# Hashed attention and a gated MLP on one core: feature rows moved to 51 to 76, the broadcast of the inverted sums in two transfers, and a new order

## The chip, the cores and the metric

The kernel runs on one core of a Trainium2 chip. The metric is the device time of one execution in microseconds (us). TensorE is PE in the profile, VectorE is DVE, ScalarE is ACT, GpSimd is POOL, and SyncE (SP) here does nothing but issue DMAs.

## The reference, cut to what matters

Each of 4 x 8 heads has 768 positions with 64 features. A position attends only to those whose six sign bits of a projection agree with its own. The result, with the heads side by side, goes through a gated MLP.

```python
q_bits = (np.einsum('bhsd,dk->bhsk', q, proj) > 0)      # and k_bits; 6 bits each
mask = q_bucket[:, :, :, None] == k_bucket[:, :, None, :]
scores = np.where(mask, scale * np.matmul(q, k.transpose(0, 1, 3, 2)), -1e9)
attn = np.exp(scores - np.max(scores, axis=-1, keepdims=True))
attn = attn / (np.sum(attn, axis=-1, keepdims=True) + 1e-09)
x = np.matmul(attn, v)                                  # to [b, 768, 512]
h = gelu(x @ w_in); u, v = h[..., :512], h[..., 512:]
out = x + (u * (w_sg @ layernorm(v, g_ln) + b_sg)) @ w_out
```

## The kernel before

**Attention.** The 32 heads are worked on as 16 pairs. The two heads of a pair lie on partitions 0 to 63 and 64 to 127, so that two matmuls over 64 rows run beside each other. For each pair:

- `load` brings q and k from HBM (L493). `parts` transposes them on PE (L529); ACT writes the high part `h` (L533) and a whole copy `x` (L542), DVE the low part `l` (L536).
- `bits` multiplies `x` by a projection `pn` on PE (L570), DVE turns the signs into features `fb` (L573), and DMAs on SP's queue carry them into the feature tile `f` (L580): eight transfers of 13 rows each, one for each of q and k, half of the positions, and head.
- `largest` makes scores with features on PE (L599) and takes row maxima on DVE (L607, L609); `shift` reduces them (`m`, L617), and small DMAs put them into one row of `f` for each head (L627).
- `weigh` makes the scores again, in nine units (L652); ACT takes the exponential into `p` (L657); PE multiplies by v (L675, L678); POOL adds the `p` up into `sum` (L687).
- `finish` comes twice for a pair, for 256 and for 512 positions: PE totals the sums (L708), ACT writes `sm` (L711), a DMA stores it to DRAM (`s`, L717), a second spreads it over partitions (`sq`, L718), DVE inverts it (L719), a third stores that (`r`, L721), and a fourth broadcasts it to `rs` (L722). Each of these waits for the one before. Then ACT (L728) and POOL (L729) read `rs`, DVE makes `xt` (L730), and a DMA stores it to `xs` in DRAM.

**MLP.** Products for the hidden layer (L901), for the gate (L1170) and for the output (L1216), from and to DRAM copies of the intermediate results.

**Order.** Each engine runs its instructions in the order in which the program gives them, and waits on semaphores. That order is made when the program is built: `Plan.order` takes every group of instructions with a priority, an assumed duration and, for DMAs, an assumed latency (`lat`), and places the group that it believes ready first. The many constants at the top are priorities and assumptions of that kind. An ACT or POOL instruction that waits for `rs` therefore holds up everything behind it on its engine.

The broadcast before is one DMA with two heads, 64 partitions each and n positions:

```python
dma(prio, 0.6, lambda eng: eng.dma_start(rs()[:, :n], rd.unsqueeze(1).broadcast_to([2, D, n])), [rb], [rs], lat=4.6 + trip)
```

At the start, `pr` (the projection) is loaded on POOL's queue (L313); ACT scales it into `pw` (L424), and `pwh`, `pwl` and `pn` follow. The six columns `fcol` come out of small matmuls (L415) and a copy on DVE (L416). Matmuls of the identity (L740) fill PE while it would stand still at the start.

Of the kernel before, what the change touches and what calls it, by code (L numbers as in the profile page):

```python
# [9 lines left out]
F32 = mybir.dt.float32  # L10
# [8 lines left out]
DRAM = bass.MemoryType.DRAM  # L19


MX = {'r0n': 3, 'zn': 3.6, 'base': 340.0, 'gs': False, 'norm': 'DVE', 'mul': ('DVE', 'DVE', 'POOL', 'POOL', 'DVE', 'POOL', 'POOL', 'POOL'), 'wg': -6.28, 'z0': -5.58, 'ox': -66.68, 'oz': -10.14, 'sp': -10.68, 'ro': -8.45, 'gr': -5.61, 'lx': 4.73, 'lz': -3.11, 'gap': 12.5, 'wo': -28.82, 'ws': 15.65, 'ul': 20.36, 'wi': -132.86, 'x0': -110.0, 'lox': ('POOL', 'DVE', 'DVE', 'DVE', 'DVE', 'POOL', 'POOL'), 'loz': ('DVE', 'POOL', 'DVE', 'POOL', 'POOL', 'POOL', 'POOL'), 'log': ('DVE', 'POOL', 'DVE', 'POOL'), 'low': ('POOL', 'DVE', 'POOL', 'DVE', 'DVE', 'DVE', 'DVE'), 'grb': 1, 'wob': 1, 'wj': -40.0}

AVP = 9.57
TRIP = 1.5
RAWS, LATEQ, PRQ = 2, 4.39, True
GY, GX, NPT = (3,), (3, 3), 14
NAV = 1
S0P = 0.76
AHEAD = 8  # L30
PREP, SHIFTP, FINP, WSTEP, WP = 0.43, -0.57, 2.66, 14.6, 17.17
LOADS = "SP"
ADDS = (["POOL", "POOL"], ["POOL", "POOL", "POOL", "POOL", "POOL"])
TAILP = -1.15
FIRSTP, FIRSTS, FIRSTQ, LATE = -3.35, 3.11, -7.41, 9.44
LOAD0 = 1.35
PARTP = 0.39
OPS = 3
VP, MARK, WARMUP = -20.0, 2, 30
X0P = 321.77  # L40
LASTADDS = ['DVE', 'POOL', 'DVE', 'DVE', 'DVE']
AHEAD1 = 3.03
BITP, BITL, FZP, XB = -16.85, 4.0, 1.42, 1
JOB0, JOBS, JOBL = 1, 108, 6.0
LOADW = 7.8
SHIFTL = 3.2
# [2 lines left out]
class Plan:  # L49
# [10 lines left out]
    TURN = 4.7  # L60
    STAY = 1.09
    BACK = 6.5
    SIDE = 1.99
    LAND = 0.62
    TAIL = {"DVE": 0.075, "ACT": 0.1, "POOL": 0.06}

# [23 lines left out]
        b.slots = slots  # L90
        return b

    def add(self, engine, cost, prio, fn, r=(), w=(), dma=0, port=None, form=None, lat=0.0):

        port = engine == "POOL" if port is None else port
        g = {"e": engine, "c": cost, "p": prio, "fn": fn, "dma": dma, "n": len(self.groups), "slots": [], "port": port, "form": form, "lat": lat}
# [24 lines left out]
        self.groups.append(g)  # L121

    def order(self):
        G = self.groups
# [31 lines left out]
        while len(out) < len(G):  # L156
# [72 lines left out]
            for m in users[n]:  # L229
                need[m] -= 1  # L230
                if n in G[m]["deps"]:
                    at[m] = max(at[m], (end if g["dma"] else free[e]) if G[m]["e"] == e and not g["dma"] else end + self.WAIT)
# [16 lines left out]
def kernel(  # L249
# [57 lines left out]

    BL, MROW = 64, 0  # L310
# [6 lines left out]

    frow = setup.tile([1, 6, P], F32, name="frow")
    nc.vector.memset(frow, 0.0)
    fv = frow[:, 0:4].rearrange("a f (b c) -> a f b c", c=BL)  # L320
    FR = 1 + NFE
    for s in range(2):
        for r in range(2):
            c0 = 1 + NB * r
            nc.vector.memset(fv[:, 2 * s, :, c0:c0 + NB], TINY if r == s else -TINY * (1.0 + 2.0 ** -23))
            nc.vector.memset(fv[:, 2 * s + 1, :, c0:c0 + NB],
                             (1.0, MISS)[s] * (1.0 if r == 0 else -1.0) * (1.0, -1.0)[s])
    nc.vector.memset(fv[:, 2, :, MROW:MROW + 1], -1.0)
    nc.vector.memset(fv[:, 3, :, MROW:MROW + 1], 1.0)
    for s in range(2):  # L330
        for f in range(2):
            for h in range(2):
                nc.gpsimd.tensor_copy(frow[:, 4 + f, 64 * s + 32 * h:64 * s + 32 * h + 2 * FR].rearrange("a (j r) -> a j r", j=2),
                                      fv[:, 2 * s + f, :, 0:FR])


    fcol = const.tile([P, 6], F32, name="fcol")

# [78 lines left out]
    pw = setup.tile([P, 2, P], F32, name="pw")  # L417
    nc.vector.memset(pw, 0.0)
    for s in range(2):
        pv = pw[:, s, :].rearrange("p (b c) -> p b c", c=BL)  # L420
        for j in range(2):
            for r in range(2):
                c0 = 1 + NB * r
                nc.scalar.mul(pv[j * D:(j + 1) * D, j, c0:c0 + NB], pr[j * D:(j + 1) * D], 1.0 if r == s else -1.0)  # L424
    pwh = const.tile([P, 2, P], F32R, name="pwh")
    pwl = const.tile([P, 2, P], F32R, name="pwl")
    nc.scalar.copy(pwh, pw)
    nc.gpsimd.tensor_sub(pwl, pw, pwh.bitcast(F32))
    pn = const.tile([P, 2, 32], F32, name="pn")
    nc.gpsimd.memset(pn, 0.0)  # L430
    for j in range(2):
        nc.gpsimd.tensor_copy(pn[j * D:(j + 1) * D, :, FR * j:FR * j + FR], pw[j * D:(j + 1) * D, :, BL * j:BL * j + FR])
# [10 lines left out]
    if True:  # L443
# [33 lines left out]
        def row(j):  # L477
            return slice(j * D, (j + 1) * D)
# [4 lines left out]
        def load(n, prio):  # L483
# [34 lines left out]
        def parts(st, i, prio):  # L518
# [3 lines left out]
            def at(t):  # L522
                return two(t()) if i == 0 else t()[:, :WIDE]
# [38 lines left out]
        def bits(st, prio):  # L562
# [50 lines left out]
        def shift(st, ph, prio):  # L613
# [78 lines left out]
        def finish(st, ph, prio):  # L692
# [599 lines left out]
```

## Time and profile before

| | |
|---|---|
| median of 3 runs | 728.65 us (725.12 to 729.06) |
| the profiled execution | 727.2 us, of which its span is 725.4 us |
| busy PE | 697.7 us, 96% of the span |
| busy DVE, POOL, ACT | 492.5, 410.4 and 384.4 us (68%, 57%, 53%) |
| DMA | 88.44 MB, mean 122 GB/s |
| longest parts of the chain that ended last | PE 65%, DMA 11% (`rs<-r` 6%), DVE 7% |

The span is from the first to the last instruction of the profiled execution; the device time around it is 1.8 us longer. Busy time of an engine counts each stretch in which at least one of its instructions runs. "Idle before" is what an engine waited before an instruction, with the instruction or DMA that ended the wait behind an arrow.

### The profile page before, as it was taken

To read this page: it belongs to the slowest core of one execution; us is meant where nothing else is said; L and a number is where in the kernel's file an instruction comes from. 1 tells how busy PE (TensorE), PEld (TensorE's weight loads), DVE (VectorE), ACT (ScalarE), POOL (GpSimd) and SP (SyncE) were. 2 spreads that over 40 slices of the span, in tenths; PEclk is the share of its full clock that TensorE was granted. 3 is DMA by queue.
4 is the path that set the end of the run, shared out by engine and by line. 5 is a ranking of instruction groups with operands and counts; after the bars stand their busy time and mean duration, and the time that the engine had idled before them with its cause. 6 is when DMAs were issued, how large, how long until landed. Compare 5 with 4: busy or idle time off the path is not lost.

```text
span 725.4 us, 16743 instructions
## 1 busy us (share of the span) xinstructions
PE 697.7 (96%) x6318; PEld 552.9 (76%) x6318; DVE 492.5 (68%) x920; ACT 384.4 (53%) x742; POOL 410.4 (57%) x371
## 2 busy tenths in 40 slices
PE   8999899899999998998998998999999999999997
PEld 7767566666665855765665658999999989899996
DVE  4987667677697676967755767748777966464343
ACT  3466456566575656665755656757668413232010
POOL 3377569668688867776966862222236553426040
PEclk9999999999999999999999999999999999999999
DMA  7523434334343344342125112799783776565433
GB/s 172 104 48 95 100 83 111 83 95 115 93 109 87 101 108 101 86 108 63 50 62 143 29 46 66 209 286 252 214 292 116 185 191 144 127 190 103 137 72 102
DMA packets 182848, 88.44 MB, mean 122 GB/s; under 512 B 148184, under 2 KB 162160, under 8 KB 182768
## 3 DMA queue, kind: packets, MB, share of 16 engines
q1 hardware_dynamic: 179600, 86.58, 45.5%
q10 hardware_dynamic: 3104, 0.80, 0.6%
q8 instruction: 50, 0.82, 0.5%
q14 instruction: 30, 0.25, 0.1%
q0 software_dynamic: 64, 0.00, 0.0%
HBM read 59.48 MB, written 25.36 MB: 117 GB/s over the span
## 4 chain that ended last, share of the span: by engine, by line
PE 65%; DMA 11%; DVE 7%; issue 6%; ACT 5%; POOL 3%; SPq 1%; ACTq 0%; POOLq 0%; DVEq 0%
PE g L1170 14%; PE g L652 13%; PE g L901 10%; PE g L1216 9%; PE g L599 6%; DMA rs<-r 6%; PE av L678 4%; PE av L675 4%; DMA sq<-s 2%; POOL sum L687 2%; ACT p L657 2%; PE g L529 2%; PE ftp L740 1%; PE g L708 1%; PE g L570 1%
## 5 line engine op out<-in xcount | busy, mean ns | idle before, releaser
L657 ACT ACTIVATE p<-g 128x512 f32<-128x512 f32 x288 | 157.0, 600 | 63.1 <-PE g L652 61.1
L687 POOL TENSOR_TENSOR sum<-sum,p 128x512 f32<-128x512 f32 x154 | 179.7, 1201 | 7.7 <-ACT p L657 7.6
L607 DVE TENSOR_REDUCE mx<-g 128x1 f32<-128x512 f32 x192 | 123.0, 684 | 22.1 <-PE g L599 18.1
L687 POOL TENSOR_TENSOR sum<-p,p 128x512 f32<-128x512 f32 x62 | 79.5, 1301 | 52.0 <-ACT p L657 52.0
L1170 PE MATMUL g<-w,op 128*128 128x384 f32 x576 | 100.6, 334 | 0.0
L1170 PEld LDWEIGHTS g<-w,op 128*128 128x128 f32 x576 | 100.0, 188 | 0.2
L675 PE MATMUL av<-p,v 128*32 128x512 f32 x768 | 88.0, 594 | 0.0
L652 PE MATMUL g<-h 64*128 64x256 f32 (+1 forms) x384 | 78.1, 358 | 6.5 <-ACT p L657 2.3
L599 PE MATMUL g<-f 64*128 64x512 f32 (+1 forms) x384 | 72.6, 348 | 1.6 <-DVE wflat L371 0.9
L652 PE MATMUL g<-f 64*128 64x256 f32 (+1 forms) x384 | 71.9, 336 | 1.9 <-DMA f<-m 1.9
L652 PE MATMUL g<-h,l 64*128 64x256 f32 (+1 forms) x384 | 73.2, 340 | 0.0
L609 DVE TENSOR_REDUCE mx<-g 128x2 f32<-128x512 f32 x96 | 61.8, 683 | 15.2 <-PE g L599 12.6
L652 PE MATMUL g<-l,h 64*128 64x256 f32 (+1 forms) x384 | 71.9, 336 | 0.0
L599 PE MATMUL g<-h 64*128 64x512 f32 (+1 forms) x384 | 70.1, 339 | 0.0
L729 POOL TENSOR_TENSOR xt<-un,rs 128x256 f32<-128x256 f32 (+1 forms) x32 | 32.5, 1016 | 59.5 <-DMA rs<-r 36.1
L901 PEld LDWEIGHTS g<-w,op 128*128 128x128 f32 x504 | 61.6, 191 | 4.3 <-issue 1.3
L901 PE MATMUL g<-w,op 128*128 128x256 f32 x504 | 63.1, 284 | 1.5 <-DVE xt L730 0.8
L652 PEld LDWEIGHTS g<-h 64*128 64x128 f32 x384 | 43.4, 187 | 27.4 <-issue 4.9
L901 PE MATMUL g<-op,w 128*128 128x384 f32 x336 | 60.3, 335 | 1.1 <-ACT out L1051 0.6
L1216 PE MATMUL g<-woh,op 128*128 128x512 f32 x192 | 60.0, 390 | 0.0
L901 PEld LDWEIGHTS g<-op,w 128*128 128x128 f32 x336 | 57.9, 188 | 1.8 <-ACT out L1051 0.9
L675 PEld LDWEIGHTS av<-p,v 128*32 128x32 f32 x768 | 23.6, 110 | 46.5 <-issue 44.4
(138 smaller groups left out, 1208.8 us busy)
## 6 DMA issues: line engine op xcount, KB each, us to landing
v<-in_v_dram SPq DMA_DIRECT2D x16, 384.0 KB
raw<-xs SPq DMA_DIRECT2D x16, 384.0 KB
vn<-out SPq DMA_DIRECT2D x24, 256.0 KB
ud<-out SPq DMA_DIRECT2D x16, 384.0 KB
ul<-ud SPq DMA_DIRECT2D x32, 192.0 KB
stg<-xs SPq DMA_DIRECT2D x96, 64.0 KB
raw<-vn SPq DMA_DIRECT2D x8, 768.0 KB
out_dram<-out SPq DMA_DIRECT2D x24, 256.0 KB
```

What stands on the lines that cost most here:

```text
L599: nc.tensor.matmul(sc[j]()[:, c * NY:c * NY + b - a], x()[row(j), 0, qs], x()[row(j), 1, a:b], start=(n == 0), stop=(n == 1))
L607: nc.vector.tensor_reduce(mx()[:, 0, i0 + w, j:j + 1], sc[j]()[:, :WIDE], axis=AX.X, op=ALU.max, negate=True)
L609: nc.vector.tensor_reduce(mx()[:, 1, i0:i0 + 2, j], two(sc[j]()), axis=AX.X, op=ALU.max, negate=True)
L652: nc.tensor.matmul(sc[j]()[:, i * w:(i + 1) * w], x()[row(j), 1, ks], y()[row(j), 0, cs], start=(m == 0), stop=(m == 3))
L657: plan.add(ACT, 0.6, prio, lambda j=j: nc.scalar.activation(p[j]()[:, :, :NY], two(sc[j]()), AF.Exp, scale=SCALE), [sc[j]], [p[j]])
L675: nc.tensor.matmul(two(av())[rows(j, a)], st.v()[:, j, x, cols(a)], ps[x][j]()[:, :, :NY], start=(x == 0), stop=(x == 5))
L678: nc.tensor.matmul(av()[rows(j, a), :NY + 1], st.v()[:, j, 2 * x + i, cols(a)], ps[x][j]()[:, i, :], start=(x == 0 and i == 0), stop=(x == ...
L687: (nc.gpsimd if e == POOL else nc.vector).tensor_add(two(sums[j]()), a, p[j]()[:, :, :NY])
L729: plan.add(POOL, 0.13 + n / 420.0, prio + TAILP, lambda: nc.gpsimd.tensor_mul(xt()[:, :n], un()[:, :n], rs()[:, :n]), [un, rs], [xt])
L901: nc.tensor.matmul(ps()[:, :n], lhs(s, i, ci, x, y), rhs(s, i, ci, x, y), start=(first and ci == 0 and x + y == 0), stop=(ci == nc_ - 1 an ...
L1170: nc.tensor.matmul(ps()[:, :HN], a()[:, x, c0:c0 + P], c()[:, 3 * HN * y + ci * HN:3 * HN * y + (ci + 1) * HN], start=(j == 0 and ci == 0 ...
L1216: nc.tensor.matmul(ps(), a()[:, x, c0:c0 + P], w()[:, 2 * j + ci, :], start=(j == 1 and ci == 0 and x == 0 and w is th), stop=(j == 0 and ...
```

## The change

- **Feature rows.** The features of the two heads lie in rows 51 to 63 and 64 to 76 of `f`, with the row of the maxima in 63 and 64, and no longer at 0 and at 64. A transfer of `bits` then takes both heads' 26 rows, so a pair needs four transfers of 26 rows and no longer eight of 13.
- **Broadcast.** `rs` is filled by two DMAs, one for each head, each from one row of `r` to 64 partitions. The second row of `f` and all sums are as before.
- **Setup.** `pw` and `pwh` are made on DVE and no longer on ACT. A small ACT instruction (`warm`) stands ahead of ACT's other work, and with it the load of the activation table.
- **Low part of pair 1** is subtracted on POOL (from `x`) and no longer on DVE.
- **Order.** The assumed latencies of the four DMAs of `finish` go from 3.6, 4.0, 4.0, 4.6 to 1.4, 2.6, 1.8, 3.2 us, consumers of `x` are assumed to wait 0.8 us longer, and some twenty priorities and engine choices have other values.

```diff
-MX = {'r0n': 3, 'zn': 3.6, 'base': 340.0, ...
+MX = {'r0n': 3, 'zn': 2.99, 'base': 340.0, ...
...
+LATS, XS = (1.4, 2.6, 1.8, 3.2), 0.8
...
+    FO, FR = D - 1 - NFE, 2 + 2 * NFE
...
-                nc.scalar.mul(pv[j * D:(j + 1) * D, j, c0:c0 + NB], pr[j * D:(j + 1) * D], 1.0 if r == s else -1.0)
+                c0 = (FO + NB - NB * r, D + 1 + NB * r)[j]
+                nc.vector.tensor_scalar_mul(pw[j * D:(j + 1) * D, s, c0:c0 + NB], pr[j * D:(j + 1) * D], 1.0 if r == s else -1.0)
...
-    nc.scalar.copy(pwh, pw)
+    nc.vector.tensor_copy(pwh, pw)
...
+                warm = late.ring([P, 1], F32, "warm")
+                plan.add(ACT, 1.4, prio + 0.5, lambda: nc.scalar.mul(warm(), small, 1.0), [], [warm])
...
+            if st.n in LOP:
+                plan.add(POOL, 1.28, prio + 0.2, low_s, [(t, x) for t in (st.x, hh) for x in keys], [(lo, x) for x in keys])
...
                     for h in range(2):
-                        for j in range(2):
-                            r = 64 * s + 32 * h + FR * j
-                            nc.sync.dma_start(ft()[j * D:j * D + FR, s, SH * h:SH * h + SH].bitcast(F32), fb()[r:r + FR, :].bitcast(F32))
-
-                plan.add(SP, 2.28, prio, spread, [fb], [(ft, (s, 0)), (ft, (s, 1))], dma=0.1, lat=BITL)
+                        r = 64 * s + 32 * h
+                        nc.sync.dma_start(ft()[FO:FO + FR, s, SH * h:SH * h + SH].bitcast(F32), fb()[r:r + FR, :].bitcast(F32))
+
+                plan.add(SP, 1.2, prio, spread, [fb], [(ft, (s, 0)), (ft, (s, 1))], dma=0.1, lat=BITL)
...
-            dma(prio, 0.6, lambda eng: eng.dma_start(rs()[:, :n], rd.unsqueeze(1).broadcast_to([2, D, n])), [rb], [rs], lat=4.6 + trip)
+            for j in range(2):
+                dma(prio, 0.6, lambda eng, j=j: eng.dma_start(rs()[row(j), :n], rd[j:j + 1].broadcast_to([D, n])), [rb], [(rs, j)], lat=LATS[3] + trip)
```

**What moves.** On SP's queue, where the broadcasts of pair 1's second half and of pair 2's first half are issued (a tile's number differs from build to build; `rs` of 512 is the second half), the order before is:

```order
L721 DMA r_1_204<-sq_1114 128x8
L718 DMA sq_1225<-s_0_205 128x4
L493 DMA k_1282<-in_k_dram 128x6x64
L722 DMA rs_1304<-r_1_204 128x1x512
L627 DMA f_199<-m_1285 1x128x2 x4
L721 DMA r_0_206<-sq_1225 128x4
L493 DMA q_1342<-in_q_dram 128x6x64 x2
L580 DMA f_200<-fb_1340 13x384 x4
L722 DMA rs_1395<-r_0_206 128x1x256
```

and of the change:

```order
L727 DMA r_1_201<-sq_1038 128x8
L361 DMA w_2_1124<-in_moe_w_in_dram 128x512
L723 DMA s_0_202<-sm_1155 4x128
L729 DMA rs_1159<-r_1_201 64x512 x2
L724 DMA sq_1187<-s_0_202 128x4
L727 DMA r_0_203<-sq_1187 128x4
L492 DMA k_1280<-in_k_dram 128x6x64
L492 DMA q_1299<-in_q_dram 128x6x64
L739 DMA xs_99<-xt_1255 128x512
L729 DMA rs_1310<-r_0_203 64x256 x2
```

Both broadcasts stand as two DMAs of 64 partitions; the first of them is now issued before the spread `sq` of the next half and before the loads of k and q, and the feature transfers have gone from between the two.

On PE, at the end of pair 2's second half (`av` is the product with v, `x` the copy that `bits` reads), the order before is:

```order
L675 MATMUL av_1287<-p_182,v_322 32x512 x2
L675 MATMUL av_1287<-p_183,v_322 32x512 x2
L570 MATMUL g_844_1320<-x_1302,pn 32x384 x4
L675 MATMUL av_1287<-p_170,v_322 32x512 x2
L675 MATMUL av_1287<-p_171,v_322 32x512 x2
```

and of the change:

```order
L681 MATMUL av_1284<-p_173,v_321 32x512 x2
L681 MATMUL av_1284<-p_174,v_321 32x512 x2
L714 MATMUL g_844_1343<-sum_1098,ones 32x256 x2
L714 MATMUL g_844_1343<-sum_1127,ones 32x256 x2
L578 MATMUL g_844_1351<-x_1297,pn 32x384 x4
```

The product for the bits has moved from the middle of the twelve `av` groups to behind all of them and behind the totals.

On DVE, at the start of the program (`p` and `mx` are tiles that are set to a constant), the order before is:

```order
L464 MEMSET mx_166 128x24
L468 MEMSET p_171 128x2
...
L468 MEMSET p_183 128x2
L416 COPY fcol<-ftp 128x6
L536 TENSOR_TENSOR l_0_306<-g_844_288,h_0_298 128x2x256
```

and of the change:

```order
L463 MEMSET mx_162 128x24
L424 TENSOR_SCALAR pw<-pr 64x6 x4
L463 MEMSET mx_163 128x24
...
L417 COPY fcol<-ftp 128x6
L424 TENSOR_SCALAR pw<-pr 64x6 x4
L427 CAST pwh<-pw 128x256
L538 TENSOR_TENSOR l_0_305<-g_844_287,h_0_297 128x2x256
```

The copy of `fcol` now stands behind the first four instructions that read `pr`.

## Rows read from the trace of the kernel before

**Rows 1.** Busy time by stage: us, each engine (instructions), PEclk, DMA share, GB/s.

```profile
25.00:425.00 400.00, 383.17 (x4381) 259.03 (x4381) 287.06 (x534) 244.86 (x485) 298.39 (x263) 0.99 0.35 88
425.00:450.00 25.00, 23.17 (x180) 16.98 (x176) 19.59 (x30) 15.97 (x31) 9.72 (x7) 1.00 0.11 33
450.00:725.00 275.00, 270.68 (x1598) 258.23 (x1597) 170.99 (x310) 115.03 (x208) 95.09 (x73) 1.00 0.64 176
```

**Rows 2.** Waits of PE from 25 to 425 us: total us, times, longest.

```profile
PE g L570 <- ACT x L542: 6.5, 9, 1.6
PE g L652 <- ACT p L657: 2.3, 2, 1.5
PE g L652 <- DMA f<-m: 1.9, 1, 1.9
PE g L652 <- DVE fb L573: 1.8, 2, 1.2
PE g L652 <- ACT sm L711: 1.6, 1, 1.6
```

**Rows 3.** Waits of the other engines from 25 to 425 us.

```profile
ACT g L728 <- DMA rs<-r: 49.0, 22, 5.6
...
DVE sq L719 <- DMA sq<-s: 23.3, 9, 4.0
```

**Rows 4.** Timeline, two broadcasts: start, duration in us, engine, line [idle before].

```profile
54.05 0.61 SPq L722 DMA_DIRECT2D rs<-r  x1
59.54 0.48 ACT L728 ACTIVATE g<-rs,less 128x256 f32<-128x256 f32 x1 [0.72 <-DMA rs<-r]
71.70 0.58 SPq L722 DMA_DIRECT2D rs<-r  x1
80.14 0.69 ACT L728 ACTIVATE g<-rs,less 128x512 f32<-128x512 f32 x1 [5.61 <-DMA rs<-r]
81.77 0.39 PE L652 MATMUL g<-h 64*128 64x256 f32 x1 [1.60 <-ACT sm L711]
```

**Rows 5.** Timeline, a small transfer issued behind a broadcast.

```profile
123.18 0.61 SPq L722 DMA_DIRECT2D rs<-r  x1
123.88 0.42 SPq L718 DMA_DIRECT2D sq<-s  x1
131.21 0.18 DVE L719 RECIPROCAL sq<-sq 128x4 f32<-128x4 f32 x1 [2.91 <-DMA sq<-s]
```

**Rows 6.** Busy time by stretch while that broadcast is under way.

```profile
127.00:128.00 1.00, 1.00 (x16) 0.27 (x10) 0.46 (x2) 1.00 (x3) 1.00 (x2) 1.00 0.84 178
128.00:130.50 2.50, 2.50 (x32) 0.91 (x28) 0.30 (x1) 0.65 (x2) 0.82 (x2) 1.00 0.19 44
```

**Rows 7.** Busy time in two stretches of lower granted clock, and before the second.

```profile
135.00:139.00 4.00, 3.25 (x23) 3.25 (x25) 3.48 (x8) 1.09 (x2) 1.20 (x2) 0.57 0.57 171
392.00:395.00 3.00, 1.06 (x6) 0.50 (x3) 0.03 (x1) 1.40 (x3) 1.33 (x2) 0.97 0.31 99
395.00:398.00 3.00, 3.00 (x17) 2.80 (x19) 2.77 (x5) 1.27 (x3) 2.28 (x2) 0.50 0.26 95
```

**Rows 8.** Timeline of PE, matmuls that wait for nothing.

```profile
78.71 0.29 PE L652 MATMUL g<-l,h 64*128 64x256 f32 x2
78.83 0.28 PE L652 MATMUL g<-f 64*128 64x256 f32 x2
```

**Rows 9.** Timeline of the start.

```profile
4.71 2.50 PE L740 MATMUL ftp<-ident 128*128 128x128 f32 x10 [0.26 <-DVE fcol L416]
5.04 1.28 ACT L424 ACT_TABLE_LOAD   x1 [5.04 <-DMA pr<-in_proj_dram]
...
19.69 0.80 DVE L557 TENSOR_SCALAR f<-g,fcol 128x512 fp32r<-128x512 f32 x1
...
21.76 0.50 PE L599 MATMUL g<-f 64*128 64x512 f32 x2
```

**Rows 10.** Instructions of L580: duration ns min/median/max, first and last start.

```profile
L580 SPq DMA_DIRECT2D f<-fb x120: 743/744/1406, 22.6 to 372.6; - x120
```

More of the change, by code (lines that the diff above doesn't have):

```diff
@@ L19 @@
 DRAM = bass.MemoryType.DRAM
-MX = {'r0n': 3, 'zn': 3.6, 'base': 340.0, 'gs': False, 'norm': 'DVE', 'mul': ('DVE', 'DVE', 'POOL', 'POOL', 'DVE', 'POOL', 'POOL', 'POOL'), 'wg': -6.28, 'z0': -5.58, 'ox': -66.68, 'oz': -10.14, 'sp': -10.68, 'ro': -8.45, 'gr': -5.61, 'lx': 4.73, 'lz': -3.11, 'gap': 12.5, 'wo': -28.82, 'ws': 15.65, 'ul': 20.36, 'wi': -132.86, 'x0': -110.0, 'lox': ('POOL', 'DVE', 'DVE', 'DVE', 'DVE', 'POOL', 'POOL'), 'loz': ('DVE', 'POOL', 'DVE', 'POOL', 'POOL', 'POOL', 'POOL'), 'log': ('DVE', 'POOL', 'DVE', 'POOL'), 'low': ('POOL', 'DVE', 'POOL', 'DVE', 'DVE', 'DVE', 'DVE'), 'grb': 1, 'wob': 1, 'wj': -40.0}
-AVP = 9.57
+MX = {'r0n': 3, 'zn': 2.99, 'base': 340.0, 'gs': False, 'norm': 'ACT', 'mul': ('DVE', 'DVE', 'POOL', 'DVE', 'DVE', 'POOL', 'POOL', 'DVE'), 'wg': -9.83, 'z0': -2.89, 'ox': -62.69, 'oz': -3.55, 'sp': -10.68, 'ro': -13.35, 'gr': -5.61, 'lx': 4.73, 'lz': -3.11, 'gap': 11.25, 'wo': -33.65, 'ws': 7.61, 'ul': 25.67, 'wi': -132.86, 'x0': -110.0, 'lox': ('POOL', 'DVE', 'POOL', 'POOL', 'DVE', 'DVE', 'DVE'), 'loz': ('DVE', 'POOL', 'DVE', 'DVE', 'POOL', 'POOL', 'POOL'), 'log': ('POOL', 'POOL', 'DVE', 'POOL'), 'low': ('POOL', 'DVE', 'POOL', 'DVE', 'DVE', 'DVE', 'DVE'), 'grb': 1, 'wob': 1, 'wj': -38.13}
+AVP = 9.1
 TRIP = 1.5
@@ L30 @@
 AHEAD = 8
-PREP, SHIFTP, FINP, WSTEP, WP = 0.43, -0.57, 2.66, 14.6, 17.17
+PREP, SHIFTP, FINP, WSTEP, WP = 0.43, -0.07, 3.42, 14.6, 19.09
 LOADS = "SP"
@@ L34 @@
 TAILP = -1.15
-FIRSTP, FIRSTS, FIRSTQ, LATE = -3.35, 3.11, -7.41, 9.44
+FIRSTP, FIRSTS, FIRSTQ, LATE = -3.35, 3.1, -7.41, 11.08
 LOAD0 = 1.35
@@ L39 @@
 VP, MARK, WARMUP = -20.0, 2, 30
-X0P = 321.77
-LASTADDS = ['DVE', 'POOL', 'DVE', 'DVE', 'DVE']
+X0P = 306.7
+LASTADDS = ['DVE', 'DVE', 'DVE', 'DVE', 'DVE']
 AHEAD1 = 3.03
-BITP, BITL, FZP, XB = -16.85, 4.0, 1.42, 1
+LOP = (1,)
+LATS, XS = (1.4, 2.6, 1.8, 3.2), 0.8
+BITP, BITL, FZP, XB = -16.85, 4.0, 1.75, 1
 JOB0, JOBS, JOBL = 1, 108, 6.0
@@ L62 @@
     BACK = 6.5
-    SIDE = 1.99
+    SIDE = 1.8
     LAND = 0.62
@@ L91, in slot, with add @@
         return b
-    def add(self, engine, cost, prio, fn, r=(), w=(), dma=0, port=None, form=None, lat=0.0):
+    def add(self, engine, cost, prio, fn, r=(), w=(), dma=0, port=None, form=None, lat=0.0, slack=0.0):
         port = engine == "POOL" if port is None else port
-        g = {"e": engine, "c": cost, "p": prio, "fn": fn, "dma": dma, "n": len(self.groups), "slots": [], "port": port, "form": form, "lat": lat}
+        g = {"e": engine, "c": cost, "p": prio, "fn": fn, "dma": dma, "n": len(self.groups), "slots": [], "port": port, "form": form, "lat": lat, "slack": slack}
         deps, after = set(), set()
@@ L231, in order @@
                 if n in G[m]["deps"]:
-                    at[m] = max(at[m], (end if g["dma"] else free[e]) if G[m]["e"] == e and not g["dma"] else end + self.WAIT)
+                    at[m] = max(at[m], (end if g["dma"] else free[e]) if G[m]["e"] == e and not g["dma"] else end + self.WAIT + g["slack"])
                 else:
@@ L306 @@
     nc.vector.memset(less, -1.0)
-    BL, MROW = 64, 0
     pr = const.tile([P, NB], F32, name="pr")
@@ L319, with span @@
     nc.vector.memset(frow, 0.0)
-    fv = frow[:, 0:4].rearrange("a f (b c) -> a f b c", c=BL)
-    FR = 1 + NFE
+    FO, FR = D - 1 - NFE, 2 + 2 * NFE
+    def span(r):
+        return slice(FO + NB - NB * r, FO + FR - NB + NB * r)
     for s in range(2):
[L323 to L329, printed above, removed]
+        for r in (1, 0):
+            nc.vector.memset(frow[:, 2 * s, span(r)], TINY if r == s else -TINY * (1.0 + 2.0 ** -23))
+            nc.vector.memset(frow[:, 2 * s + 1, span(r)], (1.0, MISS)[s] * (1.0 if r == 0 else -1.0) * (1.0, -1.0)[s])
+        for f, x in ((0, -1.0 * s), (1, 1.0 * s)):
+            nc.vector.memset(frow[:, 2 * s + f, D - 1:D + 1], x)
     for s in range(2):
         for f in range(2):
-            for h in range(2):
-                nc.gpsimd.tensor_copy(frow[:, 4 + f, 64 * s + 32 * h:64 * s + 32 * h + 2 * FR].rearrange("a (j r) -> a j r", j=2),
-                                      fv[:, 2 * s + f, :, 0:FR])
+            nc.gpsimd.tensor_copy(frow[:, 4 + f, D * s:D * s + D].rearrange("a (h r) -> a h r", h=2)[:, :, 0:FR],
+                                  frow[:, 2 * s + f:2 * s + f + 1, FO:FO + FR].broadcast_to([1, 2, FR]))
     fcol = const.tile([P, 6], F32, name="fcol")
@@ L497, in load @@
                 st.raw.append(t)
+            if n == 0:
+                warm = late.ring([P, 1], F32, "warm")
+                plan.add(ACT, 1.4, prio + 0.5, lambda: nc.scalar.mul(warm(), small, 1.0), [], [warm])
             i = (NPAIR - 1 - n) % 3
@@ L541, in parts, with low_s @@
             if st.n:
-                plan.add(ACT, 0.6, prio + 0.2, lambda: nc.scalar.copy(st.x()[:, ss, cs], at(tp)), [tp], [(st.x, x) for x in keys])
-            plan.add(DVE, 0.69, prio, low, [tp] + [(hh, x) for x in keys], [(lo, x) for x in keys])
+                plan.add(ACT, 0.6, prio + 0.2, lambda: nc.scalar.copy(st.x()[:, ss, cs], at(tp)), [tp], [(st.x, x) for x in keys], slack=XS)
+            def low_s():
+                nc.gpsimd.tensor_sub(lo()[:, ss, cs], st.x()[:, ss, cs], hh()[:, ss, cs].bitcast(F32))
+            if st.n in LOP:
+                plan.add(POOL, 1.28, prio + 0.2, low_s, [(t, x) for t in (st.x, hh) for x in keys], [(lo, x) for x in keys])
+            else:
+                plan.add(DVE, 0.69, prio, low, [tp] + [(hh, x) for x in keys], [(lo, x) for x in keys])
         def features(st, i, prio):
```

14 lines of the change are left out of this document (5 added, 9 removed).

## The prediction, made before the changed kernel ran

> **What bounds the kernel now.** I read the busy time by stage first. From 25 to 425 us, the attention, PE is busy 383.17 of 400 us, and the next engine, POOL, 298.39 [rows 1]. From 450 us on, PE is busy 270.68 of 275 us [rows 1], and part of the rest is the tail behind its last matmul. So PE's work sets the time, and a change that takes no matmul away can win only what PE loses between them. In the attention that is 400 - 383.17 = 16.8 us of idle time, and two things that the busy time hides, worked out below.
>
> Next come the waits of PE. The longest group is L570, the bits' product, which waits for the copy `x` on ACT nine times, 6.5 us [rows 2]. The other waits are 16.8 - 6.5 = 10.3 us together, of which the rows show four kinds with six waits, each in the neighbourhood of ACT or of a small DMA [rows 2].
>
> Then what holds up ACT. Its largest outside wait is for the broadcast `rs`: 49.0 us in 22 times; DVE waits 23.3 us for `sq` [rows 3]. ACT is far from full, but it runs in order: the exponentials behind the waiting instruction come late, and PE, which needs their PSUM tiles and the `sm` behind them, stops. One case: the broadcast is issued at 71.70, ACT stands 5.61 us until 80.14, and PE stands 1.60 us for `sm`, until 81.77 [rows 4].
>
> **Why the broadcast is late.** 128 KB (256 positions) issued at 54.05 are read at 59.54, 5.5 us later; 256 KB issued at 71.70 are read at 80.14, 8.4 us later [rows 4]. The second 128 KB thus cost 2.95 us, 44 GB/s, and 5.5 - 2.95 = 2.5 us are fixed. While another broadcast is under way nearly alone, the DMA engines move the same 44 GB/s at a busy share of 0.19; just before, with a load beside it, 178 GB/s at 0.84 [rows 6]. So the broadcast runs on few of the 16 engines, and what is issued behind it waits on them: `sq`, a transfer of 2 KB, issued 0.7 us behind a broadcast, is read by DVE 7.3 us later, after a wait of 2.91 us [rows 5].
>
> The Trainium skill (DMA: Bandwidth & Descriptors, section "Why a DMA increments its semaphore by 16 and not by 1") gives a reason: a DMA is spread over the largest number of engines, up to 16, that divides the slowest dimension of both sides. The old source has 2 there, the new one 64 on both sides, so 2 engines become 16. The share of 0.19 agrees [rows 6]: a little over two of sixteen.
>
> **The change part by part.** The sum is made against the profiled execution's own 727.2 us (span 725.4 and 1.8 around it); the median of the runs is 1.4 us above that, and I add this at the end.
>
> *The broadcast in two.* At the 178 GB/s that the engines reach with a load on all of them [rows 6], the second head's 128 KB take 0.74 us. With one more issue of 0.6 us [rows 4] and the fixed 2.5 us, `rs` of 512 positions is there 3.8 us after the first issue and no longer 8.4; `rs` of 256 after 3.5 and no longer 5.5. The bound on the other side is that both halves still run at 44 GB/s: 8.4 us as now. By the skill's rule it would be eight times 44 GB/s and 0.4 us sooner still, an estimate that does not alter the sum, since the wait is gone by either.
>
> The new order assumes 3.2 us where the old one assumed 4.6, and pulls the readers of `rs` forward accordingly, so there is hardly a margin. I allow each of the 32 broadcasts 0.5 us of waiting on ACT, 16 us. Before, 49.0 us of such waits [rows 3] went with 10.3 us of PE's other waits, 0.21 us for each. So of 10.3 us 3.4 come back: **-6.9 us**. Bounds: -10.3 with no wait left, 0 if as much comes back.
>
> *The bits' product.* Before, it stands in the middle of the `av` groups and waits for `x`; in the new order six more groups and the totals lie between. This takes all of its waits: **-6.5 us**; above, -3 if `x` itself comes later in ACT's order.
>
> *Refilling.* A matmul that lasts 0.28 us starts 0.12 us behind the one before when nothing waits [rows 8], so each wait also costs the 0.16 us of overlap, which counts as busy. The rows show 15 waits [rows 2]: 15 x 0.16 = 2.4 us. With three quarters of them gone: **-1.8 us** (0 to -2.4).
>
> *The clock.* In two stretches the granted clock is at or near the lower of its two levels, 1.2 instead of 2.4 GHz: four microseconds at 0.57 and three at 0.50 [rows 7], which lose 4 x 0.43 + 3 x 0.5 = 3.2 us of PE's work. Ahead of the second, PE was busy only 1.06 of 3 us [rows 7]. If the long waits go, so does this; I take half: **-1.6 us** (0 to -3.2).
>
> *The feature transfers.* 120 issues of 0.743 us [rows 10] become 60 of 26 rows: SP's queue gets 44.6 us back and spends 32 x 0.6 = 19 us on the second halves of the broadcast. No row prices an issue of 26 rows; it lies between 0.743 us and twice that, where nothing would be saved. I take the lower, since 128 rows are issued in 0.6 us [rows 4]. On the path it counts nothing either way: SP issues ahead of need. If that cover went, the transfers behind would come 0.6 us later per broadcast, within the allowance above.
>
> *The start.* The fill on PE begins right behind `fcol`, at 4.71; `pr` lands at 5.04 [rows 9]. In the new order four instructions that read `pr` stand ahead of `fcol` on DVE, and with the small ones behind them the fill begins about 5.8, and the transposes behind it come up to 1.1 us later. Against this, the last features are written by 19.69 + 0.80 = 20.5, and the maxima start only at 21.76 [rows 9], behind the bits' product; now they come first, 1.2 us sooner. The `pw` work leaves ACT, which was not late there, and pair 1's low part leaves DVE for a POOL that has nothing to add yet. Together **0** (-1.2 to +1.1).
>
> *The MLP.* Its edits move work between DVE and POOL beside a PE that is busy 98% [rows 1]: **0**. The stretch from 425 to 450 us has 1.8 us of PE's idle time [rows 1], the most that could be won or, I take it, lost there.
>
> Sum: 727.2 - 6.9 - 6.5 - 1.8 - 1.6 = 710.4, and with 1.4 for the median 711.8: I predict **712 us**. All gains at their ends (-10.3, -6.5, -2.4, -3.2, -1.2, -1.8) give 727.2 - 25.4 + 1.4 = 703; half of the gain gives 720.
>
> **The rivals.**
>
> *New waits take half or more of it back.* POOL, busy 298.39 of 400 us [rows 1], has its adds in bursts, and with PE faster the `p` tiles may come free too late. It speaks for it that everything around `finish` is pulled closer together; against it that a quarter of POOL's time is free. 8.4 us or less of gain: 720 to 725.
>
> *The change doesn't do what it says: the broadcast lands no sooner.* 64 reads of one row of DRAM, not the engines, would then be what limits it to 44 GB/s. Its reader, moved forward by the 1.4 us that the order assumes, waits so much longer 32 times: 45 us of ACT, at 0.21 us each 9.4 us of PE, against 6.5 and 1.8 saved at the bits' product: 727.2 + 9.4 - 8.3 + 1.4 = 730, within what I call no change. The rate of 178 GB/s beside it [rows 6] speaks against this, since that load reached it through the same queue.
>
> *Slower: DVE becomes the bound by its wait for `sq`.* `sq` is now assumed at 2.6 us and no longer 4.0, and DVE takes it in order, ahead of row maxima for which PE waits. DVE is busy 287.06 of 400 us [rows 1], and PE's own work there is some 383 us, so 96 us are free: from 3 us at each of the 32 it decides. At the 4.0 us that is the longest wait now [rows 3] it is 128 us, 287 + 128 = 415 us for the stretch, 15 us more than now: 744. Against it: the long waits for `sq` are those behind a broadcast [rows 5], which gets short.
>
> **How the numbers follow.** A difference under 0.5%, 3.6 us, can hardly be told from none here. Chances: the forecast, 703 to 720: 0.72; half or less of the gain, 720 to 725: 0.16; about 730 or otherwise no change: 0.08; slower through DVE or another such wait: 0.04. So faster 0.88, same 0.08, slower 0.04. The range goes from 702, a microsecond below all gains at their ends, to 723, which takes in more than half of the second case: about 0.8.
>
> **What would show it.** Right: the wait of ACT for `rs` falls from 49.0 us to under 20, that of DVE for `sq` from 23.3 to under 10; L570 leaves the list of PE's waits; PE's idle time from 25 us to the end of the attention falls to about 5 us; the granted clock stays at its upper level; `rs` is read within 4 us of its first issue, for both sizes. The attention ends some 17 us sooner, and the stretch behind it lasts as long as now. Wrong: `rs` of 512 still takes 8 us; or it takes 4 and PE still idles as much, because it waits for the adds on POOL or for DVE's maxima; or the start loses more than 1 us.

## The result, and the profile after

The changed kernel takes 704.5 us (median of 4 runs, 703.6 to 705.8), the kernel before on the same chip 728.6 us: ratio 0.968, interval 0.965 to 0.972. I had predicted 712 us, with a range of 702 to 723.

The profiled execution of the changed kernel took 704.2 us, with a span of 702.4 us; that of before 727.2 and 725.4. From the first matmul of `weigh` to the start of its last unit, busy time after (the first row) and before (the second), with the columns of [rows 1]:

```profile
24.30:402.70 378.40, 376.28 (x4420) 257.00 (x4416) 290.29 (x538) 244.93 (x486) 300.40 (x265) 1.00 0.36 94
```

```profile
22.80:425.70 402.90, 386.07 (x4418) 261.62 (x4416) 289.75 (x538) 246.62 (x488) 298.39 (x263) 0.99 0.35 88
```

The stretch is 24.5 us shorter. PE's idle time in it fell from 16.8 to 2.1 us, and its busy time, for as many matmuls, by 9.8 us. The stretch begins 1.5 us later than before, and from its end to PE's last matmul there is the same time (from 402.7 to its start at 698.3, against 425.7 to 721.1): 24.5 - 1.5 = 23.0 us, the whole difference of the spans.

All waits of PE from 25 to 405 us (total us, times, longest), against [rows 2]:

```profile
PE g L658 <- DVE fb L581: 1.0, 3, 0.5
PE g L531 <- DVE mx L614: 0.5, 2, 0.3
PE g L714 <- DVE mx L614: 0.3, 1, 0.3
PE g L606 <- DVE mx L614: 0.2, 1, 0.2
```

The bits' product (now L578) is gone from the list. The waits of ACT, DVE and POOL for small DMAs in the same window, against [rows 3]:

```profile
ACT g L735 <- DMA rs<-r: 2.5, 3, 1.1
```

```profile
DVE sq L725 <- DMA sq<-s: 3.6, 5, 1.0
```

```profile
POOL xt L736 <- DMA rs<-r: 21.9, 10, 3.9
```

ACT waits 2.5 us for the broadcast and no longer 49.0. POOL still waits 21.9 us for it, and no wait of PE leads to POOL. One broadcast of 512 positions with a spread `sq` behind it, from the timelines of SP, ACT and DVE:

```profile
189.88 1.15 SPq L729 DMA_DIRECT2D rs<-r  x2
191.11 0.54 SPq L724 DMA_DIRECT2D sq<-s  x1
```

```profile
193.40 0.69 ACT L735 ACTIVATE g<-rs,less 128x512 f32<-128x512 f32 x1 [0.72 <-DMA rs<-r]
```

```profile
193.48 0.18 DVE L725 RECIPROCAL sq<-sq 128x4 f32<-128x4 f32 x1 [0.73 <-DMA sq<-s]
```

Both readers stand waiting, so both times are those of the DMAs: 3.5 us from the first issue of the broadcast, where [rows 4] had 8.4, and 2.4 us for `sq`, where [rows 5] had 7.3.

The start, against [rows 9]:

```profile
5.05 1.58 DVE L424 TENSOR_SCALAR pw<-pr 64x6 f32<-64x6 f32 x4 [2.48 <-DMA pr<-in_proj_dram]
...
6.65 0.16 DVE L417 COPY fcol<-ftp 128x6 f32<-128x6 f32 x1
...
6.87 2.50 PE L747 MATMUL ftp<-ident 128*128 128x128 f32 x10 [2.91 <-DVE fcol L417]
```

PE stands 2.91 us for `fcol`, which stands behind four readers of `pr`; its fill begins at 6.87 and no longer at 4.71.

### The profile page after: what moved, and what is told of

Same layout as the page of the kernel before. It is cut to its first block, busy times and chain, and to the rows that moved or that the text cites. A ratio compares the mean times of both kernels' runs of the same rounds, so it can differ in the third digit from the quotient of the medians.

```text
span 702.4 us, 16712 instructions
## 1 busy us (share of the span) xinstructions
PE 688.1 (98%) x6318; PEld 549.8 (78%) x6318; DVE 506.9 (72%) x938; ACT 381.1 (54%) x734; POOL 407.0 (58%) x359
## 4 chain that ended last, share of the span: by engine, by line
PE 87%; DVE 5%; DMA 3%; ACT 2%; issue 1%; POOL 1%; SPq 0%; DVEq 0%; ACTq 0%; POOLq 0%
PE g L658 17%; PE g L908 15%; PE g L1177 14%; PE av L681 10%; PE g L1223 9%; PE g L606 9%; PE av L684 5%; PE g L531 3%; PE g L714 2%; PE ftp L747 1%; PE g L578 1%; DMA r<-sq 1%; ACT p L663 1%; DVE l L538 1%; DMA sq<-s 1%
## 5 line engine op out<-in xcount | busy, mean ns | idle before, releaser
L681 PE MATMUL av<-p,v 128*32 128x512 f32 x768 | 85.7, 594 | 0.0
L658 PE MATMUL g<-h 64*128 64x256 f32 (+1 forms) x384 | 71.9, 349 | 1.0 <-DVE fb L581 1.0
L606 PE MATMUL g<-f 64*128 64x512 f32 (+1 forms) x384 | 68.3, 346 | 0.2 <-DVE mx L614 0.2
L658 PE MATMUL g<-h,l 64*128 64x256 f32 (+1 forms) x384 | 68.4, 335 | 0.0
L658 PE MATMUL g<-f 64*128 64x256 f32 (+1 forms) x384 | 68.3, 333 | 0.0
L658 PE MATMUL g<-l,h 64*128 64x256 f32 (+1 forms) x384 | 67.8, 332 | 0.0
L606 PE MATMUL g<-h 64*128 64x512 f32 (+1 forms) x384 | 66.4, 335 | 0.0
L736 POOL TENSOR_TENSOR xt<-un,rs 128x256 f32<-128x256 f32 (+1 forms) x32 | 35.9, 1124 | 33.2 <-DMA rs<-r 21.9
L658 PEld LDWEIGHTS g<-h 64*128 64x128 f32 x384 | 39.5, 185 | 18.4 <-DVE wflat L372 4.4
```

The costliest lines, as they stand in the source:

```text
L606: nc.tensor.matmul(sc[j]()[:, c * NY:c * NY + b - a], x()[row(j), 0, qs], x()[row(j), 1, a:b], start=(n == 0), stop=(n == 1))
L658: nc.tensor.matmul(sc[j]()[:, i * w:(i + 1) * w], x()[row(j), 1, ks], y()[row(j), 0, cs], start=(m == 0), stop=(m == 3))
L681: nc.tensor.matmul(two(av())[rows(j, a)], st.v()[:, j, x, cols(a)], ps[x][j]()[:, :, :NY], start=(x == 0), stop=(x == 5))
L736: plan.add(POOL, 0.13 + n / 420.0, prio + TAILP, lambda: nc.gpsimd.tensor_mul(xt()[:, :n], un()[:, :n], rs()[:, :n]), [un, rs], [xt])
```

## The experiments

Two theories at first. **Engines**: the old broadcast is slow because it runs on few DMA engines; the split gives the gain, and the new order can stand on it only because it is fast. **Order**: the new order gives the gain by itself, and the broadcast is a side matter. Ratios are to the kernel before on the same chip (728.5 to 730.9 us there).

### One half alone, and the other

The changed kernel in its order, with the old single DMA:

```diff
-dma(prio, 0.6, lambda eng, j=j: eng.dma_start(rs()[row(j), :n], rd[j:j + 1].broadcast_to([D, n])), ...)
+dma(prio, 0.6, lambda eng, j=j: j or eng.dma_start(rs()[:, :n], rd.unsqueeze(1).broadcast_to([2, D, n])), ...)
```

> The changed kernel with its order, but the inverted sums broadcast in one transfer of two heads as before. If the late broadcast is what cost PE its time (theory), rs of 512 positions is again read some 8 us after its issue; the new order places its readers for 3.8 us, so ACT waits for rs at least the 49 us of before, probably 60 to 100 us, and the time is 722 to 735 us. If the new order alone brings the gain (rival), ACT's wait costs little and the time stays at 704 to 709 us.

Measured: 748.8 us, ratio 1.024 (1.019 to 1.030). Slower than before, and by more than I expected. The longest group of PE's waits, the one of DVE for `sq`, and one case:

```profile
PE g L531 <- DVE mx L614: 27.6, 12, 4.6
```

```profile
DVE sq L725 <- DMA sq<-s: 38.1, 15, 5.1
```

```profile
94.26 0.60 SPq L729 DMA_DIRECT2D rs<-r  x1
94.96 0.42 SPq L724 DMA_DIRECT2D sq<-s  x1
```

```profile
102.16 0.18 DVE L725 RECIPROCAL sq<-sq 128x4 f32<-128x4 f32 x1 [4.10 <-DMA sq<-s]
102.25 0.66 DVE L614 TENSOR_REDUCE mx<-g 128x1 f32<-128x512 f32 x1
```

```profile
102.97 1.11 PE L531 MATMUL g<-ident,k 128*128 128x128 f32 x4 [3.53 <-DVE mx L614]
```

`sq`, issued 0.7 us behind the broadcast, is there 7.2 us later. DVE stands for it in order; the row maxima behind it come late, and PE's transposes (L531), which need the PSUM tile that a maximum frees, stand 3.53 us. This is the prediction's third rival, with the old broadcast in place of the new one.

The kernel before in its order, with the broadcast in two:

```diff
-dma(prio, 0.6, lambda eng: eng.dma_start(rs()[:, :n], rd.unsqueeze(1).broadcast_to([2, D, n])), [rb], [rs], lat=4.6 + trip)
+def spread_rs(eng):
+    for j in range(2):
+        eng.dma_start(rs()[row(j), :n], rd[j:j + 1].broadcast_to([D, n]))
+dma(prio, 0.6, spread_rs, [rb], [rs], lat=4.6 + trip)
```

> The kernel before with its order on every engine, but the broadcast in two transfers of one head each, issued back to back. Theory (late broadcast): rs is read within 4 us, ACT's wait for it falls from 49 us to under 15, the waits of PE other than for x fall from 10 to about 3 us and the low clock goes; the bits' product still waits for x, 6 us. Time 714 to 720 us. Rival (order alone): the time stays at 725 to 729 us.

Measured: 711.5 us, ratio 0.975 (0.971 to 0.978). Four fifths of the whole gain with none of the new order. (The profiled execution was the slowest of its four, 714.8 us.) PE's waits there:

```profile
PE g L570 <- ACT x L542: 3.8, 7, 0.7
PE g L652 <- DVE mx L609: 2.6, 2, 1.8
PE g L652 <- DVE fb L573: 0.6, 1, 0.6
```

The bits' product still waits, 3.8 us where it was 6.5. The theory of the order alone is out.

### Two transfers, or the slowest dimension?

The split may help because there are two DMAs, or because each has 64 and not 2 as its slowest dimension. The changed kernel, two DMAs, each of both heads and half of the columns:

```diff
-eng.dma_start(rs()[row(j), :n], rd[j:j + 1].broadcast_to([D, n]))
+eng.dma_start(rs()[:, n // 2 * j:n // 2 * (j + 1)], rd[:, n // 2 * j:n // 2 * (j + 1)].unsqueeze(1).broadcast_to([2, D, n // 2]))
```

> The changed kernel with two transfers per broadcast, but each takes both heads and half of the positions, so the outermost dimension of the source is 2 in both, as it was in the one transfer of before. If the number of engines follows from that dimension (theory), each half runs at about 44 GB/s on the same two engines, rs of 512 is read 8 to 9 us after the first issue, and the time is that of the new order with one broadcast, 722 to 735 us. If it is the splitting into two transfers that helps (rival), it is 704 to 707 us.

Measured: 776.4 us, ratio 1.063 (1.059 to 1.067), far outside both numbers. SP, ACT, and the DMA share while such a broadcast is alone:

```profile
181.86 1.19 SPq L729 DMA_DIRECT2D rs<-r  x2
```

```profile
190.34 0.69 ACT L735 ACTIVATE g<-rs,less 128x512 f32<-128x512 f32 x1 [5.24 <-DMA rs<-r]
```

```profile
185.00:190.00 5.00, 1.49 (x20) 1.12 (x16) 0.18 (x1) 0.11 (x1) 0.00 (x0) 1.00 0.13 38
```

8.5 us for the same bytes in as many transfers as in the changed kernel, which needs 3.5; 38 GB/s at a share of 0.13, two of sixteen engines. (The prediction's 0.19 is three of sixteen and not "a little over two"; this row is the clearer one.) So the slowest dimension sets the speed, not the number of DMAs. The Trainium skill (DMA: Bandwidth & Descriptors, section "Why a DMA increments its semaphore by 16 and not by 1") says just this: the engine count is the largest one, up to 16, that divides the slowest dimensions; the run agrees.

Why 776.4 and not some 749: the two halves land 0.9 us later than the one broadcast of the first experiment (median of 15 that ACT waited for in either run: 8.55 against 7.63 us), and PE's wait by the same path, 27.6 us there, is longer:

```profile
PE g L531 <- DVE mx L614: 41.3, 12, 5.0
```

### Does `sq` wait for the engines or in SP's queue?

As the first experiment, but with `sq` issued by ACT:

```diff
-eng.dma_start(sq()[:, :W], sd.rearrange("a (p c) -> (a p) c", c=W))
+nc.scalar.dma_start(sq()[:, :W], sd.rearrange("a (p c) -> (a p) c", c=W))
```

> The changed kernel with the single broadcast as before, and the small spread sq issued by ACT and not by SP, so that the two share no queue of issues. It says nothing on the time of the whole (ACT now waits 32 times for the store ahead of sq, and the whole may well be slower than the 748.8 us of the single broadcast). What is read is the time from the issue of sq to its use on DVE where a broadcast was issued up to 2.5 us before it, some 7 us with both on SP. Theory (sq waits on the DMA engines that the broadcast occupies): still 6 us or more. Rival (sq waits behind the broadcast in SP's queue): under 4 us, as without a broadcast ahead of it.

Measured: 745.1 us (two runs), ratio 1.020 (1.013 to 1.027). SP, ACT and DVE in one case:

```profile
118.36 0.60 SPq L729 DMA_DIRECT2D rs<-r  x1
```

```profile
120.00 0.33 ACTq L724 DMA_DIRECT2D sq<-s  x1
...
125.69 0.69 ACT L735 ACTIVATE g<-rs,less 128x512 f32<-128x512 f32 x1 [2.11 <-DMA rs<-r]
```

```profile
125.20 0.18 DVE L725 RECIPROCAL sq<-sq 128x4 f32<-128x4 f32 x1 [1.54 <-DMA sq<-s]
```

Of `sq` that DVE waited for behind a broadcast there are 13 in either run: median 5.2 us from issue to use here, 6.8 with both on SP. That lies between my two numbers. But here `sq` is issued some 0.7 us later, and it still comes only about when the broadcast does: DVE reads `sq` 0.5 us before ACT reads the broadcast (medians), and with both on SP 0.1 us after. That is nothing like the 2.4 us of the changed kernel. So most of the wait stands on the DMA engines, and at most some 0.9 us of it (6.85 against 7.75 us from the issue of the broadcast) is SP's queue. The Trainium skill (DMA: Bandwidth & Descriptors, section "Queues, rings and completion order") has a rule for it: a DMA's semaphore step lands only after every earlier write of that DMA engine, whatever queue it came from. That `sq` lands so close to the broadcast, from either queue, fits the rule.

### The short latencies without the rest

The kernel before with the broadcast in two and only the four short latencies (1.4, 2.6, 1.8 and 3.2); the order is then made anew:

```diff
-dma(prio, 0.1, lambda eng: eng.dma_start(sd, sm()[0:P:32, :h]), [sm], [sb], lat=3.6 + trip)
+dma(prio, 0.1, lambda eng: eng.dma_start(sd, sm()[0:P:32, :h]), [sm], [sb], lat=1.4 + trip)
...
```

> The kernel before with the broadcast in two transfers and, in the planner, only the four assumed latencies of the finish changed to 1.4, 2.6, 1.8, 3.2; all other constants, the features and the setup as before; the order is made anew from them. Theory: the rest of the gain over e2 comes from an order that fits the latencies, so 708 to 715 us, with the waits for x left if the bits' product stays between the av groups. Rival (the other constants were tuned together with the order and matter more): no better than e2, 715 to 725 us.

Measured: 728.1 us, ratio 0.998 (0.995 to 1.001), as slow as before; worse than either theory said. DVE's and ACT's waits:

```profile
DVE sq L719 <- DMA sq<-s: 32.4, 19, 3.9
```

```profile
ACT g L729 <- DMA rs<-r: 25.8, 15, 5.7
```

The short latencies were not true in that program. I looked for what makes them true among the edits that I had put at nothing: the feature transfers.

### Eight feature transfers in the new order

```diff
-nc.sync.dma_start(ft()[FO:FO + FR, s, ...], fb()[r:r + FR, :])
+for j in range(2):
+    a, g = FO + FR // 2 * j, r + FR // 2 * j
+    nc.sync.dma_start(ft()[a:a + FR // 2, s, ...], fb()[g:g + FR // 2, :])
```

> The changed kernel with eight feature transfers of 13 rows a pair and no longer four of 26, same rows of the tile, same order. SP's queue spends 60 x 0.74 = 45 us more. My sum put this at nothing: 704 to 706 us, within 0.3% of the changed kernel. Rival: the queue is late enough that what stands behind the features (maxima rows, sums, broadcast) comes up to 3 us later in each pair and PE waits; 708 us or more.

Measured: 731.4 us, ratio 1.003 (1.001 to 1.006). All of the gain is gone. PE's and DVE's longest waits:

```profile
PE g L531 <- DVE mx L616: 11.9, 13, 3.5
PE g L716 <- DVE mx L616: 5.6, 6, 1.8
```

```profile
DVE sq L727 <- DMA sq<-s: 38.6, 28, 4.6
```

SP's queue in one place in the changed kernel, and the same place here, with DVE's wait behind it:

```profile
57.20 0.57 SPq L723 DMA_DIRECT2D s<-sm  x1
57.87 3.26 SPq L587 DMA_DIRECT2D f<-fb  x4
61.23 0.45 SPq L724 DMA_DIRECT2D sq<-s  x1
```

```profile
60.29 0.57 SPq L725 DMA_DIRECT2D s<-sm  x1
61.38 6.44 SPq L589 DMA_DIRECT2D f<-fb  x8
67.86 1.01 SPq L726 DMA_DIRECT2D sq<-s  x1
```

```profile
70.10 0.20 DVE L727 RECIPROCAL sq<-sq 128x8 f32<-128x8 f32 x1 [4.59 <-DMA sq<-s]
```

In the new order the feature transfers stand on SP between the store `s` and the spread `sq`. Four take 3.26 us there, eight 6.44, and `sq` goes out that much later; DVE, which takes `sq` in order, stands 4.59 us.

Is it SP's time, or the small transfers themselves? The same, with the second of each two issued by ACT:

```diff
-nc.sync.dma_start(ft()[a:a + FR // 2, s, ...], fb()[g:g + FR // 2, :])
+(nc.scalar if j else nc.sync).dma_start(ft()[a:a + FR // 2, s, ...], fb()[g:g + FR // 2, :])
```

> The changed kernel with eight feature transfers a pair, of which the second of each two is issued by ACT and not by SP. Theory (the cost of the eight transfers, some 27 us, is SP's time to issue them, some 0.7 us each ahead of sq in its queue): most of it comes back, 704 to 712 us, some of it lost to ACT's own time for 60 issues; DVE's wait for sq, 38.6 us with all eight on SP, falls under 20. Rival (the cost is that of small transfers on the DMA engines): 725 to 733 us as with all on SP.

Measured: 734.4 us, ratio 1.006 (1.004 to 1.008). The wait itself answers the theory, the time does not:

```profile
DVE sq L727 <- DMA sq<-s: 2.1, 2, 1.6
```

```profile
PE g L608 <- ACT p L665: 15.9, 23, 1.4
```

```profile
ACT p L665 <- DMA f<-fb: 14.1, 6, 2.8
```

DVE's wait for `sq` fell from 38.6 to 2.1 us, so that wait was SP's issue time. But ACT now issues 60 transfers of 0.78 us (47 us) and waits for their inputs in its order, its exponentials come late, and PE stands for them. The price moved to another engine in order and was no smaller.

Four transfers in the old order (the kernel before with the broadcast in two, as above, and also the new layout):

```diff
-for j in range(2):
-    r = 64 * s + 32 * h + FR * j
-    nc.sync.dma_start(ft()[j * D:j * D + FR, s, SH * h:SH * h + SH].bitcast(F32), fb()[r:r + FR, :].bitcast(F32))
+r = 64 * s + 32 * h
+nc.sync.dma_start(ft()[FO:FO + FR, s, SH * h:SH * h + SH].bitcast(F32), fb()[r:r + FR, :].bitcast(F32))
```

> The kernel before, its order on PE and ACT kept, with the broadcast in two transfers and also the features laid side by side and sent in four transfers a pair instead of eight. Alone, the broadcast in two gave 711.5 in this order. Theory (the long queue of issues on SP hurts only where the order assumes short latencies, and the old order assumes long ones): 709 to 713 us, within 0.4% of that kernel; DVE's wait for sq (20.7 us there) falls, PE's idle time does not. Rival (the four transfers are worth some 27 us by themselves, whatever the order): clearly under 705 us.

Measured: 706.9 us, ratio 0.968 (0.965 to 0.972). Somewhat under my range, but 4.6 us from the 711.5 with eight, not 27. DVE's wait for `sq` fell from 20.7 to 5.1 us, PE's waits other than for `x` from 3.5 to 0.3 us, and the bits' product waits as before:

```profile
PE g L567 <- ACT x L539: 3.8, 7, 0.7
PE av L673 <- ACT un L709: 0.3, 1, 0.3
```

With the two edits of the transfers, the old order thus reaches the ratio of the whole change, 0.968 (706.9 us here, 704.5 there, on two chips). The stretch of `weigh`, with the columns of [rows 1]:

```profile
22.10:404.20 382.10, 377.74 (x4418) 254.78 (x4416) 289.00 (x538) 245.90 (x488) 298.41 (x263) 1.00 0.37 93
```

It is 20.8 us shorter than before, of the 24.5 us in the changed kernel. What is left of the change, the new order above all, takes 3.7 us more off the attention (382.1 to 378.4) and begins it 2.2 us later (24.3 against 22.1).

And the short latencies with four transfers, but with the old other constants:

```diff
-AVP = 9.1
+AVP = 9.57
...
-X0P = 306.7
+X0P = 321.77
...
-LATS, XS = (1.4, 2.6, 1.8, 3.2), 0.8
+LATS, XS = (1.4, 2.6, 1.8, 3.2), 0.0
```

> The changed kernel with the old constants of the order, but the new short latencies, and so an order of its own; broadcast in two, four feature transfers, set-up as changed. The old kernel with the broadcast in two and the short latencies gave 728. Theory (eight feature transfers are what the short latencies could not bear): 706 to 715 us. Rival (the rest of the constants in the new order is what makes the short latencies pay): 720 us or more.

Measured: 710.4 us, ratio 0.974 (0.971 to 0.977), against 728.1 with eight transfers: that fits the theory that they are what the short latencies needed. It is not a test of one edit, since this run has also the new set-up, and an order made with 1.2 and not 2.28 us of SP for the transfers; the test of one edit is the 731.4 us above. The other constants are worth the rest, 710.4 to 704.5, and about half of that lies behind the attention: from the start of the last unit of `weigh` to that of PE's last matmul it takes 298.7 us here, and 295.6 in the changed kernel.

### The start

The changed kernel with `pw` and `pwh` on ACT as before, and with only the copy `fcol` on ACT:

```diff
-nc.vector.tensor_scalar_mul(pw[...], pr[...], 1.0 if r == s else -1.0)
-nc.vector.tensor_copy(pwh, pw)
+nc.scalar.mul(pw[...], pr[...], 1.0 if r == s else -1.0)
+nc.scalar.copy(pwh, pw)
```

```diff
-nc.vector.tensor_copy(fcol, ftp[:, 0:6])
+nc.scalar.copy(fcol, ftp[:, 0:6])
```

> The changed kernel with pw and pwh made on ACT as before, behind the early table load; DVE's copy of fcol no longer stands behind the instructions that read pr. Theory (the start is later by this alone): the fill on PE begins at about 4 us instead of 6.9, the first transposes at about 7 instead of 9.2, everything moves by some 2 us, 702 to 703 us. Rival (the loads of q and k set the start): no change, 704 to 705 us.

> The changed kernel with one line changed: the copy of fcol runs on ACT, which is idle there, and no longer on DVE behind the reads of pr. Theory: as e6, the first transposes at about 7 us, 702 to 703 us. Rival (loads): 704 to 705 us.

> The changed kernel itself, beside the three others on the same chip: 704 to 705 us, first transposes at 9.2 us.

Measured: 702.4 us (700.8 to 702.9) and 702.5 us (702.1 to 703.5), against 704.7 us (703.5 to 706.5) for the changed kernel on the same chip. In the second the fill begins when it did in the first (4.22):

```profile
4.23 2.50 PE L747 MATMUL ftp<-ident 128*128 128x128 f32 x10 [0.25 <-ACT fcol L417]
```

Both beat the changed kernel by some 2.2 us, 0.3%. It is little, but no run of the first reaches those of the changed kernel on that chip, and those of the second just touch them (703.48 and 703.45).

## Why the prediction was right, and where it was off

The direction and its main reason hold; 712 was 7.5 us too high. The parts were further off than the sum. I had priced the transfers, with refilling and clock, at 10.3 us, and in the old order they are worth 23.1 (730.0 to 706.9); I had priced the new order at 6.5 us, and the attention shows 3.7 for it. That one error makes up for a part of the other is luck.

- **The reason for the late broadcast** was right, and the split by columns shows it: the slowest dimension of 2 and not the number of transfers. Rival "the broadcast lands no sooner" is out (3.5 us). But its price was read off one long case: of the 12 broadcasts of 512 positions that ACT waited for before, 8.4 us is the second longest and 7.8 the median, and for 256 the median is 5.5. By the medians the second 128 KB cost 2.3 us and not 2.95, the fixed part is 3.2 us, and my sum would have given 4.5 us; that the 3.8 came so near to 3.5 is in part luck too.
- **"The broadcast in two", -6.9 us, was mis-sized.** In the old order, the only place where it can be seen alone, it is worth 19.5 us in medians (730.9 to 711.5), or 12.4 us from one profiled execution to the other; with refilling and clock I had some 10. I had priced it by 0.21 us of PE per us of ACT's waiting and let a third come back; nothing came back.
- **The bits' product, -6.5 us**, was right in the sum: the wait is gone in the new order, and in the old order with both other edits it is 3.8 us. So the order takes 3.8 of it and the fast broadcast the rest, which agrees with the 3.7 us of the two stretches.
- **The clock, -1.6 us**, was half of what the attention won. By single microseconds of granted clock, 3.4 us were lost before; after, none from 24 to 412 us. But a little later, when PE had just stood 2.53 us for DVE, the granted clock is at its lower level again (0.50 from 420.7 to 424.1 us), which loses 1.7 us; before, the passage to the MLP had no such stretch. Over the whole run it is 1.7 us won, and "the granted clock stays at its upper level" held in the attention alone.
- **Refilling, -1.8 us**, fell short, if it is that. PE's busy time for the same matmuls fell by 9.8 us; with 3.4 for the clock, 6.4 are left, where my bound was 2.4. My rows showed 15 waits of PE, the whole list has 21, and 7 are left after: by my price 2.2 us. What the other 4 us are, no run settles. Most of the fall comes with the transfers, since PE's busy time is already 377.74 us with both of them in the old order. And in the run with the old constants PE waits for nothing in the whole stretch and is still busy for 380.5 us with the same matmuls, so the busy time hides more than my two terms.
- **"The feature transfers ... on the path it counts nothing either way" was the step that failed.** An issue of 26 rows takes 0.78 us (60 of them, 0.743 to 1.118), as I took it. But I judged SP by its free time, in the order of before. In the new order the issues stand between two links of a chain, and twice as many cost 26.7 us (731.4 against 704.7 for the changed kernel on that chip). In the old order, which assumes longer latencies, they cost 4.6 us.
- **The start, 0, was off by 1.5 us**, more than the 1 us that I had named as a sign of being wrong: the fill began at 6.87 and not at 5.8, because the four readers of `pr` took 1.58 us. The two last kernels show it worth some 2.2 us.
- **The MLP, 0**, was right: as long after as before, the 1.7 us of the clock included.
- **The rival "new waits take half or more of it back"** is out: PE idles 2.1 us, where I had forecast some 5, and waits for POOL nowhere.
- **The slower rival's mechanism is real.** DVE's wait for `sq` stands behind the loss in three runs of the new order: with one broadcast, with the split by columns and with eight feature transfers (38.1, 49.8 and 38.6 us of it). In the changed kernel, with the fast broadcast and the short queue on SP, it is 3.6 us in all.

The edits don't add up. With four transfers in the new order, the split is worth 44 us (748.8 to 704.5); in the old order with eight, 19.5.

## What to carry to other kernels

When an order is made from assumed latencies, make the transfers fast first. The fast broadcast and the short queue of issues gave nearly all of the gain in the old order (706.9 us, against 704.5 for the whole change); the short assumptions lost it where one of the two was missing (748.8 us with the old broadcast, 728.1 and 731.4 us with eight feature transfers). So before you shorten an assumption, ask all that must hold for it to be true. Judge a queue of issues not by its free time, but by what stands between two links of a chain in the new order. A broadcast to many partitions should have the partitions, not a pair of heads, as its slowest dimension.

## What was not expected of the hardware

- A small transfer issued by ACT while a slow broadcast from SP is under way still takes 5.2 us (median of 13), against 6.8 from SP's own queue and 2.4 behind a fast broadcast: another issuing engine was little help.
- Two DMAs with a slowest dimension of 2 take 8.5 us for 256 KB, more than a single one (medians of those that ACT waited for: 8.55 against 7.6 to 7.8).
- A transfer of 26 rows takes SP nearly as long to issue as one of 13 (0.780 and 0.744 us), so half as many transfers are half the queue.
